# Backward pass of a pre-LN decode block: a thirteenth 8 KiB tile, twelve kept V, the activation's row form, and gK in the light iteration

## The chip, the cores and the metric

The kernel runs on one core of a Trainium2 chip. The metric is the device time of one execution in microseconds. Engines are called PE (matrix products, with PEld for its weight loads), DVE (VectorE), ACT (ScalarE), POOL (GpSimd) and SP (SyncE, which here only issues DMAs). All DMAs of the core share 16 DMA engines.

## The reference

One decode step (one token) of a block with attention over a cache and a ReLU MLP, and the gradients of all its inputs for a given gradient of the output:

```python
def _A_ref(x, k_cache, v_cache, wq, wo):          # B=2, Sq=1, D=640, H=32, Sk=4096, Dh=128
    q = (x @ wq).reshape(B, Sq, H, Dh).transpose(0, 2, 1, 3)
    scores = jnp.einsum("bhqd,bhkd->bhqk", q, k_cache) * (Dh ** -0.5)
    p = softmax(scores)
    o = jnp.einsum("bhqk,bhkd->bhqd", p, v_cache)
    return o.transpose(0, 2, 1, 3).reshape(B, Sq, H * Dh) @ wo

def _B_ref(x, w1, w2):                            # Dff=1728
    return jnp.maximum(x @ w1, 0) @ w2

h  = x + _A_ref(layernorm(x), k_cache, v_cache, wq, wo)
h2 = h + _B_ref(layernorm(h), w1, w2)
_out, _vjp = jax.vjp(f, A_x, A_k_cache, A_v_cache, A_wq, A_wo, B_w1, B_w2)
return (_out, *_vjp(grad_out))
```

All arrays are bf16. K and V caches are 2 x 32 heads of 4096 x 128, 1 MiB each, so 128 MiB are read at least once, and the gradients of both caches, another 128 MiB, are written.

## The kernel before

A head's K or V is one tile of 128 x 32 x 128 bf16, 8 KiB in each partition. Twelve such tiles (NBIG, L80) live in one pool; each belongs for the time being to a use: `ld` (loads), `g` (outputs gK and gV), `f` (weight gradients), `q` (weights and rows of the end). `take` and `give` (L94 to L117) hand them out and back, `share` (L123) says how many each use should own, and `more_home` adds tiles when other pools are released.

**First pass** (`p1_iter`, L448). Iteration i works on three heads at once: the scores of head i (K transposed in four groups by `pair_transpose`, L418, then `pair_matvec`, L431), the softmax of head i-1 and its product with K (`pk`, two halves, DVE), and the product of that with V of head i-2 (`m_part`). An iteration has eight parts, k = 0 to 7, and between them other work is let in. The row maximum `rmax` is made by DVE in part 6 and used by PE in part 1 of the next iteration. Transposed groups land in `t_sb`, five buffers.

**Second pass** (`p2_iter`, L836). Turn j works on one head: V is transposed again and multiplied with the output's gradient, and two outer products are written out: gV (from `rb` and the copy `pp` of P) and gK (from `rb` and `gsp`). Both are 1 MiB, made by DVE in two halves (`outer_half`, L815; in some turns ACT makes the last eight columns of gV) and issued by POOL. gK of turn j-1 is made at the beginning of turn j. V is read a second time (`Wt`), except for heads that keep theirs: KEPT = (6, 5), six in the first batch and five in the second.

**Order.** The plan (from L1062) runs first-pass iterations alone up to i = 40; from P2_AT = 41 a second-pass turn starts with every other iteration. I call an iteration in which a turn starts heavy and the one after it light. Parts of the turn are let in after parts 1 (two of them), 3, 4 and 6 of the heavy iteration (MIXED, L1112), and the turn's last part after part 1 of the light one (REST, L1113). After the first pass the turns run alone (j = 12 and up). Loads are queued in the order of the plan and issued by SP as soon as an `ld` tile is free (`pump`).

**Background.** Three lists of generators are let in at rates: the middle of a batch (`middle_gen`, L719: sum over wo, LayerNorm, w1, the gradient of the MLP, then `go_group`, whose products over wo give each head's output gradient), the weight gradients (`fin_gen`, L939, by `outer_rows`, L910), and the gradient of x (`gx_gen`, L953). In the middle of the second batch, L753 to L760 compute the activation a second time from w1 with rows in another order (`arow`, row p of column cf is p*13 + cf), which `mlp_out` (L694) needs for its loads of w2. Products with accumulation over a row (`ttr`, L641) write a `junk` tile. `bcast_cols` (L615) turns columns into rows that are equal in all partitions: `gbc`, `fbc`, `hbc`. `store_row` (L633) writes the two small outputs through `orow`, two buffers.

The first loads, `xr` from A_x and grad_out, are issued by SP (L210, L211), then five tiles of wq (L378), then K and V.

Of the kernel before, what the change touches and what calls it, by code (L numbers as in the profile page):

```python
# [15 lines left out]
def kernel(  # L16
# [20 lines left out]
    nc = tc.nc  # L37
# [18 lines left out]
    NMT = (32, 12)  # L56
# [23 lines left out]
    NBIG = 12  # L80
# [76 lines left out]
    sel = const.tile([128, 2, 2, 64], BF16)  # L157
    nc.gpsimd.memset(sel[:], 0.0)
    for par in range(2):
        nc.gpsimd.affine_select(out=sel[:, par, :, :], in_=sel[:, par, :, :], compare_op=ALU.not_equal,  # L160
                                fill=1.0, base=-par, pattern=[[0, 2], [-2, 64]], channel_multiplier=1)
# [17 lines left out]
    xr = cols.tile([4 * ND, 128], BF16)  # L179
# [15 lines left out]

    gom = cols.tile([128, H, B, 2, 2], BF16)
# [3 lines left out]
    Uc = cols.tile([128, B, H], FP32)  # L200
# [3 lines left out]
    P_bf = cols.tile([128, B * H, NSC], BF16)  # L204
# [5 lines left out]
    nc.sync.dma_start(out=xr[0:2 * ND, :], in_=A_x.rearrange("b s (c p) -> (b s c) p", p=128))  # L210
    nc.sync.dma_start(out=xr[2 * ND:4 * ND, :], in_=grad_out.rearrange("b s (c p) -> (b s c) p", p=128))  # L211
# [11 lines left out]
    def ln_fwd(xs, nb, xh, rstd):  # L223

        def st(name, dt=FP32):
            return small.tile([128, nb], dt, tag=f"ln_{name}{nb}", bufs=1, name=f"ln_{name}")
# [7 lines left out]
        cent = small.tile([128, nb, ND], FP32, tag=f"ln_cent{nb}", bufs=1, name="ln_cent")  # L234
        nc.vector.tensor_tensor(out=cent[:], in0=xs, in1=bc(mean[:], ND), op=ALU.subtract)
        sq = small.tile([128, nb, ND], FP32, tag=f"ln_sq{nb}", bufs=1, name="ln_sq")
# [5 lines left out]
        y_bf = small.tile([128, nb, ND], BF16, tag=f"ln_y{nb}", bufs=1, name="ln_y")  # L242
# [33 lines left out]
    def ln_bwd(gh, xh, rstd, add, dst, nb):  # L276

        def t3(name):
            return small.tile([128, nb, ND], FP32, tag=f"lb_{name}{nb}", bufs=1, name=f"lb_{name}")
# [35 lines left out]
    nc.tensor.transpose(x_ps[:], xr[:], ident_bf[0:4 * ND, 0:4 * ND])  # L315
# [18 lines left out]
    def pair_rows(dst, src, hs, bs):  # L334

        n, nb = hs.stop - hs.start, bs.stop - bs.start
        t = pst([128, 2, n, nb], FP32, "mid", "pr_ps")
        for par in range(2):
            nc.tensor.matmul(t[:, par, :, :], lhsT=sel[:, par, :, :].rearrange("p c k -> p (c k)"),
                             rhs=src[:, hs, bs], start=True, stop=True)  # L340
        for c in range(2):
            rows = slice(64 * c, 64 * c + 64)
            for par in range(2):
                nc.vector.tensor_copy(out=dst[rows, hs, bs, par, c], in_=t[rows, par, :, :])
# [26 lines left out]
    def all_q():  # L371

        zero = small.tile([128, H * B], BF16, tag="zero", bufs=1, name="zero")
        nc.vector.memset(zero[:], 0.0)
# [7 lines left out]
        nc.tensor.matmul(q_ps[:].rearrange("p h b -> p (h b)"), lhsT=ident_bf[:], rhs=zero[:], start=True, stop=False)  # L382
# [12 lines left out]
    KEPT = (6, 5)  # L395
# [4 lines left out]
    u4 = cols.tile([128, 128], FP32)  # L400
# [14 lines left out]
    def pair_transpose(nat, g, dve=False, busy=0):  # L415
# [8 lines left out]
        t_sb = mats.tile([128, GT // 2, 128], FP32, tag="XT", bufs=5, name="t_sb")  # L424
# [24 lines left out]
    def p1_iter(i, dve_group, busy):  # L449
# [48 lines left out]
        if p is not None:  # L498

            bp, hp = pairs[i - 1]  # L500
            bhp = bp * H + hp
# [41 lines left out]
        if p is not None:  # L543
# [3 lines left out]
            (nc.gpsimd if i < P2_AT else nc.vector).tensor_copy(out=P_bf[:, bhp, :], in_=ep[:, :, 0])  # L547
# [60 lines left out]
    def u_out(b):  # L608

        t = pst([128, H], FP32, "mid", "uc_ps")  # L610
        nc.tensor.matmul(t[:], lhsT=u4[:], rhs=fold[:], start=True, stop=True)
        nc.vector.tensor_tensor(out=Uc[:, b, :], in0=t[:], in1=rt[:, b, :], op=ALU.mult)


    def bcast_cols(colsrc, n, kc_of, dst):  # L615

        for c0 in range(0, n, 4):
            t = pst([128, 512], FP32, "bc", "bc_ps")
            w = 0
            for c in range(c0, min(n, c0 + 4)):  # L620
# [4 lines left out]
            nc.scalar.copy(out=dst[:, c0 * 128:c0 * 128 + w], in_=t[:, 0:w])  # L625
            yield
# [6 lines left out]
    def store_row(col_bf, n, dst):  # L633
# [3 lines left out]
        r = small.tile([16, 128], BF16, tag="orow", bufs=2, name="orow")  # L637
# [3 lines left out]
    def ttr(in0, in1, acc, width, kc=128, junk=None):  # L641
        if junk is None:
            junk = cols.tile([128, D], BF16, tag="junk", name="junk")
# [14 lines left out]
    def go_group(b, h0, h1, hbc):  # L658
# [4 lines left out]
        for k in range(n):  # L663
            yield from turn()
            ttr(wo_t[:, h0 + k, :], hbc[:], go32[:, k:k + 1], D)
# [16 lines left out]
        nc.vector.tensor_tensor(out=ud[:, 0:n], in0=Uc[:, b, hs], in1=negdot[:, hs, b], op=ALU.mult)  # L682
# [8 lines left out]
    def mlp_out():  # L691
# [3 lines left out]
        for k in range(NW2):  # L695
            while free["q"] < 1:
                yield
# [21 lines left out]
    def middle_gen(b):  # L719
        if o_next[0] < (b + 1) * H // OG:  # L720
            o_group()
        nc.vector.tensor_reduce(out=u4[:], in_=u_bank[0][:].rearrange("p (s d) -> p d s", s=4),
# [28 lines left out]
        if b == B - 1:  # L751
            ar_ps = pst([128, NFF, B], FP32, "mid", "ar_ps")
            for cf in range(NFF):  # L753
                for c in range(ND):
                    nc.tensor.matmul(ar_ps[:, cf, :], lhsT=w1_t[:, c, bass.ds(cf, 128, step=NFF)],
                                     rhs=x2c[:, c, :], start=(c == 0), stop=(c == ND - 1))
                yield 0.25
            nc.vector.tensor_scalar(out=arow[:, 0:NFF, :], in0=ar_ps[:], scalar1=0.0, scalar2=None, op0=ALU.max)
            if F_rem:
                nc.vector.tensor_copy(out=arow[:, NFF, :], in_=acol[:, NFF, :])  # L760
# [4 lines left out]
        fbc = cols.tile([128, Dff], BF16, tag="fbc", name="fbc")  # L765
        gx2 = small.tile([128, 1, ND], FP32, tag="gx2", bufs=1, name="gx2")
        gx2p = small.tile([128, ND, 3], FP32, tag="gx2p", bufs=1, name="gx2p")
        FW = Dff // 3
        spread_f = bcast_cols(one(ghfc, b), NF, f_kc, fbc)
        have = 0  # L770
        for k in range(3):
            while have < min(Dff, (k + 1) * FW):
                next(spread_f)
                have += 512
                yield
            for c in range(ND):
                yield from turn()
                ttr(w1_t[:, c, k * FW:(k + 1) * FW], fbc[:, k * FW:(k + 1) * FW], gx2p[:, c, k:k + 1], FW)
# [4 lines left out]
        hbc = cols.tile([128, D], BF16, tag="rowbc", name="hbc")  # L783
        yield from bcast_cols(one(gh1c, b), ND, lambda c: 128, hbc)
# [10 lines left out]
    def ga_gen():  # L795

        gbc = cols.tile([128, Dff], BF16, tag="fbc", name="gbc")
        for b in range(B):
            yield from bcast_cols(one(gc, b), ND, lambda c: 128, gbc[:, b * D:(b + 1) * D])
        for k in range(NW2):  # L800
# [3 lines left out]
            for c in range(k * FP, min(NF, (k + 1) * FP)):  # L804
                kc = f_kc(c)
                for b in range(B):
                    yield from turn()
                    ttr(t[0:kc, c - k * FP, :], gbc[0:kc, b * D:(b + 1) * D], ga[0:kc, b, c:c + 1], D, kc)
# [14 lines left out]

    def p2_iter(j, busy, act=0):

        c = S2[j] if j < NP1 else None
        p = S2[j - 1] if j >= 1 else None
        if p is not None:
            bp, hp = turns[j - 1]
            pair_matvec(p["dp"], p.pop("T3"), 3, gom[:, hp, bp, :, :])  # L830
            gsp = small.tile([128, NSC, 2], BF16, tag="gsp", name="gsp")
            nc.vector.scalar_tensor_tensor(  # L832
                out=gsp[:], in0=p["dp"][:, :, None].to_broadcast([128, NSC, 2]), scalar=negdot[:, hp, bp:bp + 1],
                in1=P_bf[:, bp * H + hp, :, None].to_broadcast([128, NSC, 2]), op0=ALU.add, op1=ALU.mult)
        if c is not None:
# [9 lines left out]
            rb = mats.tile([128, 256], BF16, tag="rb", bufs=4, name="rb")  # L845
            nc.scalar.activation(out=rb[:], in_=bank[:, 128:384], func=ACT.Copy, scale=rt[:, b, h:h + 1])  # L846
            pp = small.tile([128, NSC, 2], BF16, tag="pp", name="pp")
            nc.gpsimd.tensor_copy(out=pp[:], in_=P_bf[:, b * H + h, :, None].to_broadcast([128, NSC, 2]))
# [391 lines left out]
```

## Time and profile before

| what | value |
|---|---|
| median of 3 runs | 902.24 us (900.63 to 907.04) |
| profiled execution, span | 902.8 us |
| PE, PEld busy | 757.2, 634.2 us |
| DVE, ACT, POOL busy | 687.2, 485.8, 198.7 us |
| moved by DMA | 362.89 MB, mean 402 GB/s |
| HBM read, written | 212.16 MB, 149.13 MB |
| loads of K, V, V again (Wt) | 64, 64, 53 of 1 MiB |
| first pass alone, both, second pass alone | 0 to about 258, to 452, to the end |

The profile comes from one execution. Its span is cut into 40 slices of 22.6 us; a digit is the busy share in tenths. The DMA row is the share of time in which the 16 engines have a packet in work, GB/s what they moved; PEclk is the clock that was granted to PE, in tenths of full speed. In a table by stretches, each engine has its busy time and in brackets its instructions. A line of the timeline gives start, duration, engine, source line, and in brackets how long the engine was idle before it and what ended that.

### The profile page before, as it was taken

To read this page: it belongs to the slowest core of one execution; us is meant where nothing else is said; L and a number is where in the kernel's file an instruction comes from. 1 tells how busy PE (TensorE), PEld (TensorE's weight loads), DVE (VectorE), ACT (ScalarE), POOL (GpSimd) and SP (SyncE) were. 2 spreads that over 40 slices of the span, in tenths; PEclk is the share of its full clock that TensorE was granted. 3 is DMA by queue.
4 is the path that set the end of the run, shared out by engine and by line. 5 is a ranking of instruction groups with operands and counts; after the bars stand their busy time and mean duration, and the time that the engine had idled before them with its cause. 6 is when DMAs were issued, how large, how long until landed. Compare 5 with 4: busy or idle time off the path is not lost.

```text
span 902.8 us, 24701 instructions
## 1 busy us (share of the span) xinstructions
PE 757.2 (84%) x10205; PEld 634.2 (70%) x10205; DVE 687.2 (76%) x1286; ACT 485.8 (54%) x1248; POOL 198.7 (22%) x349
## 2 busy tenths in 40 slices
PE   3999899899999898898968876878999778959880
PEld 3888788888888787787757765656767566645560
DVE  2566788777988796697778697769798448999982
ACT  0444344344565554464536677776577656637660
POOL 1344444343311011010012141122112111111120
PEclk9999999999999999798985555555557555555555
DMA  8999999999879999999999999999999999999995
GB/s 365 426 419 414 417 402 417 424 424 377 330 310 381 415 405 424 425 416 425 404 399 399 389 410 417 417 389 388 404 413 409 425 424 424 419 425 422 423 422 240
DMA packets 56256, 362.89 MB, mean 402 GB/s; under 512 B 5680, under 2 KB 11696, under 8 KB 15312
## 3 DMA queue, kind: packets, MB, share of 16 engines
q1 hardware_dynamic: 34704, 212.18, 57.8%
q0 software_dynamic: 18432, 134.23, 35.9%
q10 hardware_dynamic: 3008, 14.91, 4.1%
q8 instruction: 80, 1.31, 0.5%
q14 instruction: 32, 0.26, 0.1%
HBM read 212.16 MB, written 149.13 MB: 400 GB/s over the span
## 4 chain that ended last, share of the span: by engine, by line
PE 49%; DMA 21%; DVE 13%; ACT 11%; issue 5%; SPq 1%; POOL 0%; ACTq 0%; POOLq 0%; DVEq 0%
PE t_ps L423 21%; PE m_ps L457 10%; DMA Vt<-in_A_v_cache_dram 10%; ACT t_sb L428 3%; ACT gV L880 3%; DMA out_dram<-gK 3%; PE s_ps L436 3%; DVE gV L819 3%; PE u_ps L486 3%; PE dp_ps L436 3%; PE o_ps L928 3%; DMA wqs<-in_A_wq_dram 3%; DVE pk L464 2%; DVE gK L819 2%; DMA Kt<-in_A_k_cache_dram 2%
## 5 line engine op out<-in xcount | busy, mean ns | idle before, releaser
L428 ACT COPY t_sb<-t_ps 128x512 f32<-128x512 f32 x479 | 273.4, 585 | 211.0 <-PE t_ps L423 205.2
L436 PEld LDWEIGHTS <-t_sb 128*128 128x128 bf16 x4096 | 181.6, 103 | 62.0 <-ACT t_sb L428 27.4
L423 PE MATMUL t_ps<-ident_f,Wt 128*128 128x128 f32 x848 | 207.2, 396 | 0.4 <-ACT t_sb L428 0.4
L457 PE MATMUL m_ps<-pk,Vt 128*128 128x129 bf16 x2048 | 171.8, 223 | 16.1 <-DMA Vt<-in_A_v_cache_dram 14.7
L464 DVE TENSOR_TENSOR pk<-Kt,ep 128x2048 bf16<-128x2048 bf16 x128 | 156.5, 1223 | 33.5 <-PE m_ps L457 15.3
L423 PEld LDWEIGHTS t_ps<-ident_f,Wt 128*128 128x128 f32 x848 | 144.1, 206 | 33.2 <-issue 27.1
L819 DVE TENSOR_TENSOR gK<-rb,gsp 128x2048 bf16<-128x2048 bf16 x128 | 152.2, 1223 | 13.1 <-DMA out_dram<-gV 10.9
L423 PE MATMUL t_ps<-ident_f,Kt 128*128 128x128 f32 x1024 | 156.7, 287 | 4.4 <-DMA Kt<-in_A_k_cache_dram 4.3
L457 PEld LDWEIGHTS <-Vt 128*128 128x128 bf16 x2048 | 125.3, 99 | 46.5 <-issue 29.7
L819 DVE TENSOR_TENSOR gV<-rb,pp 128x2048 bf16<-128x2048 bf16 (+1 forms) x128 | 142.9, 1140 | 10.9 <-DMA out_dram<-gK 6.0
L423 PEld LDWEIGHTS t_ps<-ident_f,Kt 128*128 128x128 f32 x1024 | 113.7, 145 | 8.5 <-PE s_ps L436 2.6
L474 POOL COPY pk<-ep 128x16 bf16<-128x16 bf16 x80 | 83.2, 1042 | 161.0 <-ACT ep L512 90.5
L436 PE MATMUL dp_ps<-gom,t_sb 128*128 128x2 bf16 x2048 | 96.6, 168 | 17.8 <-ACT t_sb L428 17.1
L881 POOL DMA_DIRECT2D out_dram<-gV x64 | 34.2, 534 | 304.7 <-DVE gV L819 175.4
L436 PE MATMUL s_ps<-qm,t_sb 128*128 128x2 bf16 x2048 | 87.7, 164 | 1.2 <-DVE t_sb L426 1.2
L860 POOL DMA_DIRECT2D out_dram<-gK x64 | 34.0, 532 | 222.0 <-DVE gK L819 167.9
L571 ACT CAST MT<-m_ps 128x128 bf16<-128x128 f32 x64 | 17.1, 267 | 104.4 <-PE m_ps L457 104.3
L934 ACT CAST ot<-o_ps 128x512 bf16<-128x512 f32 (+4 forms) x160 | 70.2, 489 | 2.9 <-DMA out_dram<-ot 1.5
L832 DVE SCALAR_TENSOR_TENSOR gsp<-dp_ps,negdot,P_bf 128x64 bf16<-128x64 f32 x64 | 18.0, 282 | 50.8 <-PE dp_ps L436 50.0
L644 DVE CUSTOM_DVE_ANT_0 junk<-wo_t,hbc 128x640 bf16<-128x640 bf16 x64 | 52.7, 823 | 0.2
L846 ACT ACTIVATE rb<-dp_ps,rt 128x256 bf16<-128x256 f32 x64 | 30.1, 470 | 41.1 <-PE dp_ps L841 40.4
L644 DVE CUSTOM_DVE_ANT_0 gxj<-wqs,gqr 128x1024 bf16<-128x1024 bf16 x40 | 48.8, 1220 | 1.5 <-DMA wqs<-in_A_wq_dram 1.3
(200 smaller groups left out, 779.0 us busy)
## 6 DMA issues: line engine op xcount, KB each, us to landing
Kt<-in_A_k_cache_dram SPq DMA_DIRECT2D x64, 1024.0 KB, 15.3
Vt<-in_A_v_cache_dram SPq DMA_DIRECT2D x64, 1024.0 KB, 15.3
out_dram<-gV POOLq DMA_DIRECT2D x64, 1024.0 KB, 13.1
out_dram<-gK POOLq DMA_DIRECT2D x64, 1024.0 KB, 13.9
Wt<-in_A_v_cache_dram SPq DMA_DIRECT2D x53, 1024.0 KB, 12.4
wq_t<-in_A_wq_dram SPq DMA_DIRECT2D x5, 1024.0 KB, 9.0
wo_t<-in_A_wo_dram SPq DMA_DIRECT2D x4, 1280.0 KB, 18.1
wqs<-in_A_wq_dram SPq DMA_DIRECT2D x5, 1024.0 KB, 17.1
```

The source lines that it names most:

```text
L423: nc.tensor.transpose(t_ps[:, j, :], natf[:, 2 * cc:2 * cc + 2, :].rearrange("p c k -> p (c k)"), ident_f[:])
L428: nc.scalar.copy(out=t_sb[:], in_=t_ps[:])
L436: nc.tensor.matmul(dst[:, sc:sc + 2], lhsT=v[:, j, :, par], rhs=vecs[:, par, :], start=(par == 0), stop=(par == 1))
L457: nc.tensor.matmul(r["m"][:, 0:129], lhsT=r["V"][:, sc, :], rhs=r["pk"][sc // HALF][:, sc % HALF, 0:129], start=(sc == 0), stop=(sc == NSC ...
L464: nc.vector.tensor_tensor(out=p["pk"][k][:, :, 0:128].rearrange("p s (a two) -> p s a two", two=2), in0=p["K"][:, sl, :].rearrange("p s (a ...
L474: nc.gpsimd.tensor_copy(out=col, in_=e)
L644: nc.vector.tensor_tensor_reduce(out=junk[0:kc, 0:width], in0=in0, in1=in1, scale=1.0, scalar=0.0, op0=ALU.mult, op1=ALU.add, accum_out=acc)
L819: nc.vector.tensor_tensor(out=pairs_view(dst[:, sl, :]), in0=row.rearrange("p (a two) -> p a two", two=2)[:, None, :, :].to_broadcast([128 ...
L846: nc.scalar.activation(out=rb[:], in_=bank[:, 128:384], func=ACT.Copy, scale=rt[:, b, h:h + 1])
L860: nc.gpsimd.dma_start(out=natural(out_2, bp, hp), in_=gK[:])
L881: nc.gpsimd.dma_start(out=natural(out_3, b, h), in_=gV[:])
L934: nc.scalar.copy(out=ot[0:P, k, n0:n0 + nn], in_=o_ps[0:P, 0:nn])
```

## The change

- NBIG is 13. The space comes from smaller buffers: P in 52 slots that are reused (`P_slot`), three rows of 640 (`rows`) in place of `xr`, `junk`, `fbc`, `gbc`, `hbc`, `zero`, `u4`, ten second-kind slots for M instead of twelve, `sel` without its doubled half, LayerNorm tiles shared by both sizes, and one buffer fewer for `t_sb` (4), `rb` (3), `pp`, `gsp` (2) and `orow` (1).
- KEPT is (6, 6). Shares of `ld` grow by one.
- gK of a turn is made in its light iteration by `p2_tail`, as long as both passes run.
- `arow` is made in `fin_gen` from the row form of the activation, by 13 small products with the identity; `mlp_out` waits for it. The gradient of w2 (out_7) is laid out by 128 rows of 13, and a rest of 64.
- The rows of the MLP's gradient come in parts of 640, 640 and 448 instead of three of 576.
- `xr` is loaded by ACT's queue.
- While the rows for the gradient of x are spread, the weight gradients go on at 0.4 of their rate.

```diff
-    NMT = (32, 12)
+    NMT = (32, 10)
-    NBIG = 12
+    NBIG = 13
-    xr = cols.tile([4 * ND, 128], BF16)
+    rows = cols.tile([128, 3, D], BF16)
+    junk_row = rows[:, 2, :]
-    P_bf = cols.tile([128, B * H, NSC], BF16)
+    NPS = 52
+    P_bf = cols.tile([128, NPS, NSC], BF16)
+    P_free = list(range(NPS))
+    P_slot = {}
-    nc.sync.dma_start(out=xr[0:2 * ND, :], ...
+    xr = rows[0:4 * ND, 0, 0:128]
+    nc.scalar.dma_start(out=xr[0:2 * ND, :], ...
...
-            nc.tensor.matmul(t[:, par, :, :], lhsT=sel[:, par, :, :].rearrange("p c k -> p (c k)"),
-                             rhs=src[:, hs, bs], start=True, stop=True)
+            for c in range(2):
+                nc.tensor.matmul(t[64 * c:64 * c + 64, par, :, :], lhsT=sel[:, par, :],
+                                 rhs=src[:, hs, bs], start=True, stop=True)
...
-    KEPT = (6, 5)
+    KEPT = (6, 6)
-    u4 = cols.tile([128, 128], FP32)
+    u4 = junk_row[:, 0:256].bitcast(FP32)
-        t_sb = mats.tile([128, GT // 2, 128], FP32, tag="XT", bufs=5, name="t_sb")
+        t_sb = mats.tile([128, GT // 2, 128], FP32, tag="XT", bufs=4, name="t_sb")
...
-        r = small.tile([16, 128], BF16, tag="orow", bufs=2, name="orow")
+        r = small.tile([16, 128], BF16, tag="orow", bufs=1, name="orow")
...
-            while free["q"] < 1:
-                yield
+            while free["q"] < 1 or "arow" not in FIN:
+                yield 0.0 if "arow" not in FIN else 0.5
...
-        if b == B - 1:
-            ar_ps = pst([128, NFF, B], FP32, "mid", "ar_ps")
-            for cf in range(NFF):
-                for c in range(ND):
-                    nc.tensor.matmul(ar_ps[:, cf, :], lhsT=w1_t[:, c, bass.ds(cf, 128, step=NFF)],
-                                     rhs=x2c[:, c, :], start=(c == 0), stop=(c == ND - 1))
-                yield 0.25
-            nc.vector.tensor_scalar(out=arow[:, 0:NFF, :], in0=ar_ps[:], scalar1=0.0, scalar2=None, op0=ALU.max)
-            if F_rem:
-                nc.vector.tensor_copy(out=arow[:, NFF, :], in_=acol[:, NFF, :])
...
+    def p2_gs(j):
+        p = S2[j]
+        bp, hp = turns[j]
+        pair_matvec(p["dp"], p.pop("T3"), 3, gom[:, hp, bp, :, :])
+        gsp = small.tile([128, NSC, 2], BF16, tag="gsp", bufs=2, name="gsp")
+        nc.vector.scalar_tensor_tensor(...)
+        P_free.append(P_slot.pop((bp, hp)))
+        return gsp
...
-        p = S2[j - 1] if j >= 1 else None
+        p = S2.get(j - 1)
...
+    def p2_tail(j):
+        p = S2[j]
+        bp, hp = turns[j]
+        gsp = p2_gs(j)
+        yield
+        gK = take("g", [128, NSC, 128], "gK")
+        outer_half(gK, p["rb"][:, 128:256], gsp, 0)
+        yield
+        outer_half(gK, p["rb"][:, 128:256], gsp, 1)
+        nc.gpsimd.dma_start(out=natural(out_2, bp, hp), in_=gK[:])
+        give(gK)
+        del S2[j]
+        yield
...
-        yield from outer_rows(FIN["ar"], Dff, FIN["gr"], D, out_7, Dff // 96)
+        yield
+        ar_ps = pst([128, NFF, B], FP32, "mid", "ar_ps")
+        for cf in range(NFF):
+            nc.tensor.matmul(ar_ps[:, cf, :], lhsT=FIN["ar"][0:B, bass.ds(cf, 128, step=NFF)],
+                             rhs=ident_bf[0:B, 0:B], start=True, stop=True)
+        nc.scalar.copy(out=arow[:, 0:NFF, :], in_=ar_ps[:])
+        nc.scalar.copy(out=arow[:, NFF, :], in_=acol[:, NFF, :])
+        FIN["arow"] = True
+        yield
+        yield from outer_rows(FIN["ar"], NFF * 128, FIN["gr"], D, out_7, NFF, F_rem)
...
-    REST = {1: 1}
+    REST = {1: 2, 4: 1, 6: 1}
+    def p2_whole(j):
+        yield from p2_iter(j, 0)
+        yield from p2_tail(j)
...
-            share(ld=8 + 3 * more, g=7 + 3 * more)
+            share(ld=9 + 3 * more, g=7 + 3 * more)
...
-            share(ld=5 + more, g=5 + 2 * more, f=3, q=2 + 3 * more)
+            share(ld=6 + more, g=5 + 2 * more, f=3, q=2 + 3 * more)
...
-            g2 = p2_iter(j, 0, 8 if i is None and j <= H else 0)
+            if i is not None and n + 1 < len(plan) and plan[n + 1][1] is None:
+                g2 = p2_whole(j)
+            else:
+                g2 = p2_iter(j, 0, 8 if i is None and j <= H else 0)
...
-                bg_step(1, RATE2)
+                bg_step(1, RATE2 * (0.4 if spreading[0] else 1.0))
```

## The prediction

> **What bounds the kernel now.** I read first the slices of the page, for the DMA engines and the granted clock:
>
> ```profile
> PEclk9999999999999999798985555555557555555555
> DMA  8999999999879999999999999999999999999995
> GB/s 365 426 419 414 417 402 417 424 424 377 330 310 381 415 405 424 425 416 425 404 399 399 389 410 417 417 389 388 404 413 409 425 424 424 419 425 422 423 422 240
> ```
>
> The DMA engines are busy nearly everywhere, and no slice moves more than 426 GB/s. I take 424 GB/s as full rate. The page's 362.89 MB would need 856 us at it, so about 47 us of the 902.8 us span are lost service, and only less data or less loss can shorten the kernel. Where it is lost, by stretches:
>
> ```profile
> 20.00:200.00 180.00, 171.81 (x2915) 151.25 (x2916) 132.35 (x242) 73.79 (x220) 74.14 (x92) 1.00 1.02 418
> 200.00:280.00 80.00, 77.01 (x1362) 68.06 (x1360) 65.24 (x170) 43.00 (x118) 18.22 (x33) 1.00 0.88 347
> 280.00:320.00 40.00, 36.01 (x579) 31.46 (x577) 32.73 (x68) 22.20 (x65) 5.25 (x8) 0.96 1.00 397
> 320.00:440.00 120.00, 107.61 (x1692) 94.47 (x1693) 91.70 (x183) 62.99 (x175) 12.87 (x21) 0.90 1.01 422
> 440.00:540.00 100.00, 77.74 (x1004) 68.99 (x1003) 79.68 (x149) 59.75 (x159) 23.63 (x46) 0.63 1.00 397
> 540.00:700.00 160.00, 132.63 (x1207) 105.66 (x1206) 128.30 (x234) 114.36 (x288) 32.57 (x71) 0.55 1.00 405
> 700.00:880.00 180.00, 146.47 (x1275) 107.52 (x1273) 145.76 (x200) 107.26 (x227) 27.34 (x59) 0.54 1.01 423
> 880.00:903.00 23.00, 1.33 (x25) 0.92 (x22) 6.15 (x7) 1.17 (x2) 1.59 (x3) 0.56 0.57 239
> ```
>
> Columns: stretch, its length, busy time of PE, its weight loads, DVE, ACT, POOL, granted clock, DMA share, GB/s. Lost against 424: 14.5 us in 200 to 280 (80 x 77/424), 2.5 in 280 to 320, 6.4 in 440 to 540, 7.2 in 540 to 700, 10 in the tail, some 6 elsewhere. From 700 to 880 nothing is lost: there time is bytes alone, so whatever the engines win earlier counts only as bytes moved before 700.
>
> In 200 to 280 it is the engines that hold DMA back: all 32 first-batch heads are done, VectorE (65.2 of 80 us busy) carries the products of the middle on top of each head, and PE waits for data for only 2.5 us between 205 and 325 (the waits). Two heads with one backward turn I call a pair. One that DMA does not delay looks like this, light iteration first, then heavy:
>
> ```profile
> 328.10:334.70 6.60, 6.60 (x107) 5.61 (x104) 6.57 (x14) 4.37 (x14) 1.71 (x2) 1.00 1.01 421
> 334.70:342.90 8.20, 7.62 (x143) 6.74 (x143) 6.37 (x13) 4.65 (x12) 0.53 (x1) 1.00 1.01 426
> ```
>
> The light one is bound by DVE (6.57 of 6.6), the heavy one by PE (7.62 of 8.2). A pair moves four tiles of K and V, one reloaded V and two outputs, 7 x 1.049 MB = 7.34 MB, 17.3 us at full rate; the first six pairs use kept V and move 6.29 MB, 14.8 us.
>
> **The change, step by step**, against the profiled span of 902.8 us (the median of three runs is 902.24, inside 900.63 to 907.04, so the differences carry over).
>
> One V fewer is reloaded: 53 loads of Wt become 52, 1.05 MB/424 = 2.5 us. It was read in a stretch that drains at full rate later, so I count all of it: -2.5 (bounds -2.5 and 0).
>
> The thirteenth tile: while the engines bind (200 to 280) loads run one tile further ahead, and when DMA binds after 325 one tile is already there: 1.05 MB again, -2.5. Bounds: 0, if the tile only fills with an idle V, and -5.0, if the lead is won a second time in 440 to 700, where 13.6 us are lost. From the 60th head on the extra kept V holds it, which the first term has paid.
>
> xr and grad_out move from SP's queue to ACT's. The first wq load was issued at 1.53 us, behind two issues that began at 0.74: -0.8, since SP issues all twelve loads of the start back to back. ACT loads its table from 0.73 to 2.01 us; should its DMAs stand behind that, x arrives some 1.3 us later, which the wq tiles hide (PE waits for wq at 11.4 anyway). Bounds -0.8 and +1.3.
>
> gK in the light iteration: gsp and two halves of gK (0.28 + 2 x 1.22 = 2.7 us of DVE), the last four transposes' products (0.4 us of PE) and one POOL issue move from the heavy to the light iteration, half a pair earlier. No instruction is added. The first outputs start some 7 us earlier, in a stretch where DMA is 0.80 to 0.88 busy: half a tile of lead on average, -1.2 (0 to -2.5). Against it, heavy falls to about 7.7 us (PE), and light grows to 6.6 + 1.5 = 8.1 us with gK's second half falling behind the next maximum, or 9.3 with both in front. I take 8.1, since the second half is issued after the maximum: a pair of 15.8 us. The first six pairs took 96.2 us (257.7 to 353.9), 16.0 each, DMA waits included; the later five 17.9. So 0; bounds -1 (six pairs at 15.8) and +6 (six pairs at 17.0). The 17.3 us of DMA covers the later ones.
>
> The second layout of the MLP activation: 65 matmuls over w1 and their wait leave the middle of batch two. They show as this DVE gap:
>
> ```profile
> 494.72 1.83 DVE L819 TENSOR_TENSOR gV<-rb,pp 128x2048 bf16<-128x2048 bf16 x2
> 502.35 0.18 DVE L758 TENSOR_SCALAR arow<-ar_ps 128x26 bf16<-128x26 f32 x1 [5.81 <-PE ar_ps L755]
> ```
>
> 5.8 us of DVE disappear; instead come 13 small matmuls and two ACT copies in the gradient's background work. DMA falls to 384 GB/s in 500 to 520 (1.9 us lost), so I take -1.9; bounds -5.8 and 0 (a wait for output tiles follows at 504 anyway). out_7 with 128 rows needs 28 pieces for 36: 8 x 0.49 us of ACT, which is 46 us idle in 540 to 700: 0 (to -3.9).
>
> One row buffer for two in store_row. The second copy now waits until the first row has left, and DVE stands:
>
> ```profile
> 804.58 0.21 DVE L638 COPY orow<-row_ps 5x128 bf16<-5x128 bf16 x1
> 804.81 1.26 SPq L639 DMA_DIRECT2D out_dram<-orow  x2
> 805.14 0.21 DVE L638 COPY orow<-row_ps 5x128 bf16<-5x128 bf16 x1 [0.36 <-PE row_ps L636]
> ```
>
> The packets of these rows start 4.8 to 11.0 us after the issue, behind reads, so DVE stands about 7 us, and behind it wait gsp, gK and gV of that turn and the gx products. DMA lives on what is queued, 4.7 MB issued and not yet moved at 805, 11 us, and DVE has 7.1 us free in 800 to 880. I take +0.7, bounds 0 and +7. The Trainium skill ("DMA: Bandwidth & Descriptors", Anatomy of one DMA) gives about 2.0 us fixed cost for a small DMA; by it the term would be 0. The trace, with its queue in front, is what I use.
>
> At nothing: t_sb with 4 buffers, since with gK moved every transpose stands behind the products of the fourth one before it in PE's own order; were gK not moved, the T3 of a turn would be held over the pair. rb 3, gsp 2, pp 2: their last readers are issued earlier on the same in-order engine. The P slots, the shared rows and halved statistics save space; one more ACT copy of 0.4 us per batch. pair_rows gets 24 matmuls of 0.17 us, in turns that wait for ACT or DMA.
>
> Sum: -2.5 -2.5 -0.8 -1.2 -1.9 +0.7 = -8.2: a span of 894.6, a time of 894.0.
>
> **Rivals.** *The lead pays more than once.* For it: 440 to 700 loses 13.6 us with queues that run dry between outputs, and 280 to 320 another 2.5. A third of these 16.1 us back besides: 894.0 - 5.4 = 888.6. Against it: PE there never waits for a reloaded V, and DVE waits for output tiles instead, of which there are no more than before. 0.25.
>
> *The lead is absorbed*: the heavier light iteration and the row wait eat it at their bounds short of that (+6, +1): 901. 0.10.
>
> *Slower: the two iterations no longer overlap and PE's clock halves in the light one.* Before, each was near both limits; now heavy waits for PE and light for DVE, once per iteration through the maximum that DVE hands to PE. Two rows show what waiting does:
>
> ```profile
> 367.50:371.00 3.50, 1.29 (x9) 0.95 (x9) 1.29 (x9) 1.07 (x2) 0.00 (x0) 0.94 1.03 433
> 371.00:375.00 4.00, 3.17 (x34) 3.11 (x35) 2.12 (x3) 1.08 (x3) 0.00 (x0) 0.50 1.01 426
> ```
>
> At half clock four transposes take 1.05 us for 0.62 (x4), eight products with V 1.05 for 0.63 (x4), u 0.98 for 0.62: +3.8 us on some 5.9 us of PE, so light is 9.7 to 10.9 us and a pair 17.4 to 18.6. That decides once light passes 17.3 - 7.7 = 9.6 us. Price: six pairs at +1.4 to +2.6 and five at up to +0.7, and no lead from tile or gK: up to 19 us, 14 as the middle; 902.2 - 2.5 - 0.8 - 1.9 + 0.7 + 14 = 912. Against it: in 334.7 to 342.9 PE kept full clock with 7.62 of 8.2 busy. 0.20. The Trainium skill ("TensorE: Matmul & The Clock Gate", Part 1) says the clock drops after an idle window of about 3.4 us; the two rows agree (1.29 of 3.5 busy, then 0.50), and by it the gaps of 2 us in a light iteration would not suffice, which leaves this rival without its second half.
>
> **Numbers.** Forecast 894.0 with 0.45, its own range 889 to 899. About 1% (9 us) is what a measurement can tell from no change: below 893.2 is faster, above 911.3 slower. Half the forecast's case lies below 893.2 (0.225), with the first rival 0.475: faster 0.48. Slower 0.20, same 0.32. Range 885 (the lead's rival with its bounds) to 908 (absorbed, with the row wait at +7): it leaves out the slower rival.
>
> **What would show it.** Right: 52 Wt loads and 361.8 MB; 200 to 320 above 375 GB/s; no DVE gap for arow, 500 to 520 above 395; pairs at 15 to 16 us before the first reload; first wq issue near 0.75; a DVE wait for an orow DMA of 4 to 11 us. Wrong: pairs above 17.3 us with clock 0.5 inside them, DMA below 400 in 320 to 440, new waits of ACT for t_sb products, or a queue that is empty after the row wait.

## The result, and the profile after

The changed kernel takes 909.64 us (median of 20 runs, 906.27 to 914.35), the kernel before 903.63 us in the same series (20 runs). The ratio is 1.0062, with a 95% interval of 1.0045 to 1.008: about 6 us slower, where 8 us less were forecast, and 1.6 us beyond the upper end of the range. The profiled execution has a span of 905.4 us.

The slices of the changed kernel's page, in the same 40 parts as before (granted clock, busy share of the DMA engines, what they moved):

```profile
PEclk9999998999999999998985555555555655555555
DMA  9999999999989999999999999999999999999977
GB/s 378 419 410 405 410 397 410 420 418 408 355 304 363 423 421 423 422 422 425 389 408 392 419 418 415 398 423 406 419 423 381 382 426 424 425 399 364 410 311 318
```

Two long places stand out against the slices before, and a short one (the 31st and 32nd slice, 679 to 724 us, with 381 and 382 for 409 and 425). From the second slice to the ninth the DMA row is full, but moves 397 to 420 GB/s, where seven of these eight had 414 to 426 before. And from the 36th slice on (792 us) it falls to 311 at the lowest, where before it stayed at 422 or more until the last slice. By stretches, with the last 205 us cut once more (columns as before: busy PE, weight loads, DVE, ACT, POOL, clock, DMA share, GB/s):

```profile
20.00:200.00 180.00, 171.18 (x2868) 149.90 (x2867) 130.68 (x238) 73.39 (x219) 72.27 (x91) 0.98 1.02 411
200.00:280.00 80.00, 75.97 (x1337) 66.94 (x1330) 64.72 (x169) 41.67 (x115) 19.36 (x34) 1.00 0.90 350
280.00:320.00 40.00, 36.57 (x639) 32.17 (x637) 33.45 (x66) 23.15 (x63) 3.15 (x7) 1.00 1.01 419
320.00:440.00 120.00, 105.57 (x1727) 92.82 (x1724) 92.73 (x190) 65.31 (x178) 9.18 (x21) 0.96 1.01 423
440.00:540.00 100.00, 74.54 (x952) 65.84 (x951) 82.96 (x160) 61.76 (x164) 23.13 (x48) 0.65 1.00 403
540.00:700.00 160.00, 125.92 (x1178) 100.22 (x1177) 122.57 (x217) 107.90 (x269) 34.24 (x68) 0.53 1.01 409
700.00:780.00 80.00, 68.50 (x621) 50.90 (x620) 64.22 (x83) 49.57 (x108) 11.95 (x26) 0.56 1.01 413
780.00:880.00 100.00, 71.05 (x567) 49.17 (x567) 76.10 (x113) 52.30 (x112) 14.21 (x31) 0.53 0.93 377
880.00:905.00 25.00, 13.72 (x126) 9.84 (x125) 12.47 (x13) 9.79 (x19) 3.39 (x8) 0.57 0.82 331
```

Between 200 and 700 us the change does what it was to do: each of the five stretches moves 1 to 22 GB/s more than before. On both sides of it something is lost: 20 to 200 has 411 for 418 (3.0 us: 180 x 7/424), 700 to 780 has 413 for 424 (2.1 us), and 780 to 880 has 377 for 422 (10.6 us). The two last stretches of the kernel before, for comparison:

```profile
700.00:780.00 80.00, 66.41 (x592) 49.31 (x591) 54.35 (x67) 48.13 (x105) 10.93 (x24) 0.52 1.01 424
780.00:880.00 100.00, 80.06 (x684) 58.21 (x682) 91.42 (x134) 59.13 (x123) 16.41 (x35) 0.56 1.01 422
```

The times of second-pass turns say the same. Turn 0 makes its rows `rb` at 259.9 us (before 257.7, so 2.2 us late), turn 52 at 778.6 (before 782.1, 3.5 us early), and the end comes 2.6 us late.

What happens at 790 us is in the timeline of DVE (start, duration, line, operation, count, and in brackets the idle time before it and what ended it):

```profile
788.24 1.22 DVE L653 CUSTOM_DVE_ANT_0 rows<-wqs,gqr 128x1024 bf16<-128x1024 bf16 x1
...
789.39 0.21 DVE L647 COPY orow<-row_ps 5x128 bf16<-5x128 bf16 x1
804.80 0.21 DVE L647 COPY orow<-row_ps 5x128 bf16<-5x128 bf16 x1 [15.21 <-DMA out_dram<-orow]
804.94 0.26 DVE L829 SCALAR_TENSOR_TENSOR gsp<-dp_ps,negdot,P_bf 128x64 bf16<-128x64 f32 x1
```

It is the wait that the prediction named, for the single row buffer, but 15.2 us long. What it does to DMA shows in the finer stretches of the changed kernel (same columns):

```profile
790.00:805.00 15.00, 6.12 (x53) 4.41 (x53) 0.20 (x2) 4.18 (x10) 0.00 (x0) 0.50 1.01 427
805.00:820.00 15.00, 11.01 (x124) 9.86 (x124) 14.90 (x22) 8.55 (x21) 2.00 (x4) 0.65 0.97 383
820.00:860.00 40.00, 27.78 (x211) 18.51 (x208) 39.59 (x60) 21.93 (x45) 7.06 (x15) 0.53 0.97 383
860.00:880.00 20.00, 18.86 (x135) 11.80 (x134) 11.96 (x16) 13.53 (x27) 3.04 (x8) 0.50 0.74 300
```

While DVE stands (0.20 us busy of 15) DMA loses nothing: 427 GB/s, out of what was queued. Afterwards DVE has almost no free time until 860 (14.90 of 15, 39.59 of 40), and DMA moves 383 GB/s. Bytes issued and not yet moved, added up from the trace's issues and packets, were 6.5 MB at 790 us and 0.76 MB at 805: the queue was used up while DVE, which makes the large outputs, stood.

Not only the outputs stood. SP issues the rows and the loads in one order, and the second row could not be issued before its copy. The timeline of SP (a line spans from the first of its issues to the end of the last):

```profile
789.62 15.71 SPq L648 DMA_DIRECT2D out_dram<-orow  x2
805.38 0.44 SPq L1008 DMA_DIRECT2D wqs<-in_A_wq_dram  x1
805.91 25.21 SPq L450 DMA_DIRECT2D Wt<-in_A_v_cache_dram  x4
```

Two loads of 1 MiB follow the second row within 0.6 us. So for 15 us neither POOL (which waits for gK) nor SP put anything large into the queue; ACT issued one output.

### The profile page after: what moved, and what is told of

Same layout as the page of the kernel before. It is cut to its first block, busy times and chain, and to the rows that moved or that the text cites. A ratio compares the mean times of both kernels' runs of the same rounds, so it can differ in the third digit from the quotient of the medians.

```text
span 905.4 us, 24731 instructions
## 1 busy us (share of the span) xinstructions
PE 750.9 (83%) x10169; PEld 625.2 (69%) x10169; DVE 685.8 (76%) x1284; ACT 486.7 (54%) x1244; POOL 193.8 (21%) x349
## 2 busy tenths in 40 slices
DMA packets 56288, 361.84 MB, mean 400 GB/s; under 512 B 5680, under 2 KB 11888, under 8 KB 15472
## 4 chain that ended last, share of the span: by engine, by line
PE 40%; DVE 22%; DMA 18%; ACT 10%; issue 7%; SPq 0%; ACTq 0%; POOL 0%; POOLq 0%; DVEq 0%
PE t_ps L429 18%; DMA Vt<-in_A_v_cache_dram 9%; PE m_ps L463 8%; DVE rows L653 7%; DVE gV L818 5%; DVE gK L818 5%; ACT gV L887 4%; DMA Kt<-in_A_k_cache_dram 4%; DVE pk L470 3%; ACT t_sb L434 3%; PE s_ps L442 3%; PE o_ps L955 2%; PE dp_ps L442 2%; PE u_ps L492 2%; DMA out_dram<-gV 2%
## 5 line engine op out<-in xcount | busy, mean ns | idle before, releaser
L434 ACT COPY t_sb<-t_ps 128x512 f32<-128x512 f32 x479 | 274.0, 588 | 204.6 <-PE t_ps L429 200.8
L429 PE MATMUL t_ps<-ident_f,Wt 128*128 128x128 f32 x832 | 202.7, 395 | 0.8 <-ACT t_sb L434 0.8
L470 DVE TENSOR_TENSOR pk<-Kt,ep 128x2048 bf16<-128x2048 bf16 x128 | 156.3, 1222 | 44.4 <-ACT ep L517 21.1
L429 PEld LDWEIGHTS t_ps<-ident_f,Wt 128*128 128x128 f32 x832 | 141.2, 206 | 32.5 <-issue 23.7
L961 ACT CAST ot<-o_ps 128x512 bf16<-128x512 f32 (+3 forms) x152 | 68.3, 490 | 5.5 <-ACT ot L961 1.9
L867 POOL DMA_DIRECT2D out_dram<-gK x53 | 28.3, 533 | 164.0 <-DVE gK L818 146.9
L653 DVE CUSTOM_DVE_ANT_0 rows<-wo_t,rows 128x640 bf16<-128x640 bf16 x64 | 52.6, 822 | 0.4 <-ACT rows L633 0.2
L653 DVE CUSTOM_DVE_ANT_0 rows<-wqs,gqr 128x1024 bf16<-128x1024 bf16 x40 | 48.8, 1220 | 0.2
```

Source lines behind the costliest of these rows:

```text
L429: nc.tensor.transpose(t_ps[:, j, :], natf[:, 2 * cc:2 * cc + 2, :].rearrange("p c k -> p (c k)"), ident_f[:])
L434: nc.scalar.copy(out=t_sb[:], in_=t_ps[:])
L470: nc.vector.tensor_tensor(out=p["pk"][k][:, :, 0:128].rearrange("p s (a two) -> p s a two", two=2), in0=p["K"][:, sl, :].rearrange("p s (a ...
L653: nc.vector.tensor_tensor_reduce(out=junk[0:kc, 0:width], in0=in0, in1=in1, scale=1.0, scalar=0.0, op0=ALU.mult, op1=ALU.add, accum_out=acc)
L961: nc.scalar.copy(out=ot[0:kp, k, n0:n0 + nn], in_=o_ps[0:kp, 0:nn])
```

## The experiments

Every kernel ran beside the kernel before on the same chip; ratios are to that, with 95% intervals. Differences between single profiles carry less than the ratios: the stretch from 200 to 280 us came out at 329 to 350 GB/s among kernels that hardly differ there (up to 4 us).

### The four output rows get places of their own

The changed kernel, where the rows no longer share one buffer but lie side by side in the junk row, which has room:

```diff
+    stored = [0]
-        r = small.tile([16, 128], BF16, tag="orow", bufs=1, name="orow")
+        r = junk_row[0:16, 128 * stored[0]:128 * stored[0] + 128]
+        stored[0] += 1
```

> The changed kernel, with the four small output rows each in a place of its own in the junk row, so that no row waits for another's DMA. Theory W (the single row buffer made the loss): the 15.2 us in which DVE stands before the second row are gone, DMA stays above 420 GB/s from 780 to 880, and the time is 898 to 902, below the kernel before (903.6). Rival L (the loss comes from the light iteration, from the t_sb buffers or from the extra kept V): the time stays at 906 to 910.

Measured: 899.3 us, ratio 0.995 (0.9926 to 0.9975). Against the changed kernel that is 1.12% less, 10.1 us. The same finer stretches of this kernel:

```profile
790.00:805.00 15.00, 10.82 (x101) 7.43 (x100) 14.22 (x22) 7.96 (x23) 1.98 (x4) 0.59 1.01 426
805.00:820.00 15.00, 11.43 (x131) 7.90 (x128) 14.90 (x21) 10.56 (x23) 2.93 (x6) 0.75 1.02 425
820.00:860.00 40.00, 28.97 (x226) 19.85 (x225) 35.68 (x54) 22.27 (x45) 6.96 (x15) 0.50 1.01 424
860.00:880.00 20.00, 18.49 (x121) 10.65 (x120) 11.28 (x14) 12.97 (x25) 2.66 (x7) 0.50 1.01 421
```

The wait is gone (DVE 14.22 of 15), SP goes on to issue `wqs` at 796.57 us and `Wt` at 802.40, and DMA holds 421 GB/s or more to 880 us. So the wait cost 10 us, more than the change as a whole lost. How much of it came through DVE's outputs and how much through SP's loads was not separated.

### The kernel before with one row buffer

```diff
-        r = small.tile([16, 128], BF16, tag="orow", bufs=2, name="orow")
+        r = small.tile([16, 128], BF16, tag="orow", bufs=1, name="orow")
```

> The kernel before, with one row buffer instead of two and nothing else changed. Theory W: DVE stands 10 to 15 us between the first two rows and the time goes up by 6 to 11 us, to 910 to 915. Rival L: within 2 us of 903.6, because the queued DMA work covers the wait.

Measured: 907.99 us, ratio 1.004 (1.0014 to 1.0066), 3.6 us (1.3 to 6.0). The middle lies between the theory's 6 to 11 us and the rival's 2, and the interval reaches to both. The timeline of DVE in this kernel:

```profile
809.05 0.21 DVE L638 COPY orow<-row_ps 5x128 bf16<-5x128 bf16 x1
820.61 0.21 DVE L638 COPY orow<-row_ps 5x128 bf16<-5x128 bf16 x1 [11.35 <-DMA out_dram<-orow]
```

The same wait, 11.35 us, without any other part of the change, and again a loss from 780 to 880 (395 GB/s for 422). It costs a third of what it does in the changed kernel. Two things differ there, a wait 4 us longer and a DVE that is then full for 55 us; which of them makes the difference was not separated.

How long a row waits can be read from the trace's records of its packets (issue to the start of the row's last packet) beside the bytes queued at about that time:

```
kernel               row issued   queued    at 424 GB/s   last packet after
before, first row    804.81 us    4.7 MB    11.2 us        7.0 us
before, second row   805.38 us    4.7 MB    11.2 us       10.4 us
after                789.62 us    6.5 MB    15.3 us       14.1 us
after, at 256 bytes  788.66 us    6.4 MB    15.0 us       14.4 us
before, one row      809.29 us    4.1 MB     9.7 us       10.4 us
own places, first    795.67 us    7.0 MB    16.5 us       11.1 us
own places, second   796.23 us    7.0 MB    16.5 us       15.8 us
```

(Queued is at the nearest of the marks 5 us apart; where two rows follow each other closely, the earlier five of the ten packets are taken for the first.) In five of the seven the last packet comes within 1.2 us of the time that the queue in front needs. The two rows of the profile before lay behind 4.7 MB; in the changed kernel the row comes 15 us earlier, behind 6.5 MB. Its last two rows, issued at 868.8 and 876.0 us when DMA had fallen to 300 GB/s, were through after 1.6 us each.

### gK in the light iteration, alone

The kernel before, with gK of a turn made by `p2_tail` in its light iteration, and nothing else:

```diff
+    def p2_tail(j):
...
-    REST = {1: 1}
+    REST = {1: 2, 4: 1, 6: 1}
...
+            if i is not None and n + 1 < len(plan) and plan[n + 1][1] is None:
+                g2 = p2_whole(j)
```

> The kernel before, with gK in the light iteration as the only change. The prediction's step (outputs half a pair earlier): -1.2, so 901 to 904. Rival L (light bound by DVE, heavy by PE, no overlap): pairs before the first reload go from 16.0 to 17 us and the time to 908 or more.

Measured: 903.41 us, ratio 0.9994 (0.9966 to 1.0023). Neither a gain of 1.2 us nor none can be told from it; a loss of the size that the slower rival needs (14 us) can be excluded.

### The activation's second layout from row form, alone

The kernel before, with `arow` from 13 products with the identity and out_7 laid out by 128 rows:

```diff
-            for cf in range(NFF):
-                for c in range(ND):
-                    nc.tensor.matmul(ar_ps[:, cf, :], lhsT=w1_t[:, c, bass.ds(cf, 128, step=NFF)],
...
+        for cf in range(NFF):
+            nc.tensor.matmul(ar_ps[:, cf, :], lhsT=FIN["ar"][0:B, bass.ds(cf, 128, step=NFF)],
+                             rhs=ident_bf[0:B, 0:B], start=True, stop=True)
...
+        yield from outer_rows(FIN["ar"], NFF * 128, FIN["gr"], D, out_7, NFF, F_rem)
```

> The kernel before, with the activation's second layout made from the row form (and out_7 by 128 rows) as the only change. The prediction's step: the 5.8 us DVE gap near 500 us is gone and the time falls by 1.9, to 901 to 902.5. Rival: the wait for output tiles that follows takes it back, 903 to 904.

Measured: 901.19 us, ratio 0.9958 (0.9933 to 0.9983): 3.8 us gained (1.5 to 6.1), twice the term of 1.9 in the middle; the interval has the term in it and passes its bound of 5.8 only just. In its profile 440 to 540 has 407 GB/s for 397 and 540 to 700 has 412 for 405 (2.4 and 2.6 us); 700 to 780 gives 3.4 back (406 for 424), and some 4 come after 880. These are readings of single profiles: 200 to 320 us, where the edit changes nothing, differs by 3.4 us the other way (337 and 381 GB/s for 347 and 397). The second stretch was counted at 0, with out_7's fewer pieces costing ACT less only where ACT is idle anyway.

### The tiles start at a multiple of 256 bytes

With own rows the kernel still read slowly from 20 to 200 us (411 GB/s). The trace's packet records show where. Nine tenths of the bytes of that stretch are packets of 8192 bytes, each one row of K, V or a weight; before, such a packet took 309 ns from the 10th to the 90th percentile, in the changed kernel 309 to 320, 312 in the middle. What is read there is the same; where the tiles lie differs. As built, the big tiles start at byte 47616 of each partition before, a multiple of 256, and at 39840 after, 160 bytes past one, since all that was made smaller lies below them. The next kernel is the one with own places for the rows (its tiles start at 39584, 160 past as well), with 96 bytes of padding, which puts them at 39680:

```diff
-    half_f32c = const.tile([128, 1], FP32)
-    nc.vector.memset(half_f32c[:], 0.5)
-    half_f32 = half_f32c[:].to_broadcast([128, 128])
+    half_f32c = const.tile([128, 32], FP32)
+    nc.vector.memset(half_f32c[:, 0:1], 0.5)
+    half_f32 = half_f32c[:, 0:1].to_broadcast([128, 128])
```

> The kernel of e1 with 96 unused bytes in each partition ahead of the big tiles, so that these start at a multiple of 256 bytes again (they start 160 bytes past one in e1 and in the changed kernel, and at a multiple before). Theory A (start address): reads of 8 KiB rows take 309 ns each again in 20 to 200 us (311 to 321 in e1), 20:100 and 100:200 move 418 GB/s instead of 411, and the time falls by 3 to 4 us below e1, to 0.991 of the kernel before. Rival R (another cause, such as the load of xr by ACT or thirteen tiles in flight): rows and rates stay as in e1, time 0.995.

Measured: 893.49 us, ratio 0.9877 (0.9844 to 0.991), faster than both kernels. Its stretches up to 440 us:

```profile
20.00:200.00 180.00, 170.55 (x2924) 149.38 (x2924) 132.72 (x240) 73.19 (x219) 74.85 (x93) 0.99 1.02 419
200.00:280.00 80.00, 75.99 (x1335) 67.20 (x1332) 63.95 (x168) 42.37 (x117) 17.71 (x31) 1.00 0.89 344
280.00:320.00 40.00, 35.76 (x605) 31.14 (x602) 34.51 (x69) 23.78 (x65) 3.14 (x7) 1.00 1.01 422
320.00:440.00 120.00, 104.80 (x1727) 91.52 (x1728) 94.00 (x197) 65.78 (x179) 9.91 (x23) 0.98 1.01 424
```

The engines' work is the same, and the first stretch moves 419 GB/s. The interval lies wholly below that of the kernel with own rows alone (0.9926 to 0.9975): 96 unused bytes are worth 0.73%, 6.6 us, where 3 to 4 were expected. The stretch from 20 to 200 us accounts for 3.4 of them (180 x 8/424); where the others arise was not shown. It is not the engines' own speed: DVE's products `pk` and gK take 1222 and 1225 ns in this kernel, 1221 and 1224 with own rows alone.

The opposite, on the kernel before: 32 bytes of padding, so that its tiles start 32 past a multiple of 256 (the same edit with 16 elements).

> The kernel before with 32 unused bytes ahead of the big tiles, nothing else changed, so that they start 32 bytes past a multiple of 256. Theory A: rows of 8 KiB take 311 to 321 ns in 20 to 200 us, the rate falls from 418 to 411, time up by 2 to 4 us (1.002 to 1.005). Rival R: 309 ns, 418 GB/s, 1.000.

Measured: 912.64 us, ratio 1.0081 (1.0046 to 1.0116), 7.3 us where 2 to 4 were expected. The row from 20 to 200 us:

```profile
20.00:200.00 180.00, 173.10 (x2848) 152.53 (x2848) 129.74 (x240) 73.38 (x219) 70.76 (x90) 0.98 1.02 410
```

So 32 bytes alone make the kernel before as slow as the whole change did. And how coarse the boundary is, by the kernel with own rows and tiles 128 bytes past a multiple of 256 (64 elements):

> The kernel of e1 with 224 unused bytes, big tiles 128 past a multiple of 256 (a multiple of 64 and 128). If only a multiple of 256 is good, rows take 311 to 321 ns and 411 GB/s as in e1; if 64 or 128 is enough, 309 ns and 418 GB/s.

A single run: 900.62 us, and

```profile
20.00:200.00 180.00, 168.92 (x2868) 147.49 (x2868) 131.09 (x238) 73.11 (x219) 73.42 (x91) 0.99 1.02 411
```

The reads stay slow: half of 256 does not help. The last of this group is the changed kernel with the padding and with its single row buffer:

> The changed kernel with 96 bytes of padding and nothing else, so that its 8 KiB tiles start at a multiple of 256 bytes (39936); the single row buffer stays. Theory (row wait and tile start are two separate losses): the wait of DVE for the first output row stays at 12 to 16 us, 8 KiB rows take 309 ns, 20 to 200 us goes back to 418 GB/s or more, and the ratio is 1.0062 - 0.0073 = 0.999 (902 to 904 us). Rival (what reads win earlier is lost again while DVE stands, since the queue only gets shorter): the ratio stays at 1.004 to 1.006 although the rows take 309 ns.

Measured: 904.5 us, ratio 0.9991 (0.9968 to 1.0013), as the first theory has it. Its two stretches that matter:

```profile
20.00:200.00 180.00, 169.42 (x2870) 147.87 (x2870) 131.02 (x238) 73.10 (x219) 73.41 (x91) 0.98 1.02 419
...
780.00:880.00 100.00, 71.77 (x574) 50.41 (x574) 75.14 (x110) 52.79 (x112) 14.03 (x30) 0.53 0.94 384
```

The early reads are back at 419, the row wait (15.4 us) and its loss stay. The two losses add: padding alone takes off 0.71%, own rows alone 1.12%, together 1.83%, and both in one kernel took off 1.85%.

### What the tile and the kept V are worth

The best kernel with five V kept in the second batch, thirteen tiles as they are:

```diff
-    KEPT = (6, 6)
+    KEPT = (6, 5)
```

> The kernel of e5 with KEPT (6, 5), so 53 reloads of V and a thirteenth tile that is free for loads. The prediction's first term: one reload more costs 2.5 us against e5. Rival: the reload falls into stretches where the engines bind, and the time is within 1 us of e5.

Measured: 895.33 us, ratio 0.989 (0.9858 to 0.9923). The intervals overlap nearly whole: 0.13%, 1.2 us by the ratios, against a term of 2.5, is not resolved. From 700 to 780 us this kernel moves 423 GB/s, and so does the next, while all five with six kept V and the slower rate have 413 or 414 (1.9 us); this would speak for a kept V that gives back part of what it saves. But from 780 to 880 the kernel with five kept moves 406 GB/s for 421 (3.5 us the other way), and these are single profiles, so it stays open. Then also without the tile:

```diff
-    NBIG = 13
+    NBIG = 12
-    KEPT = (6, 6)
+    KEPT = (6, 5)
...
-            share(ld=9 + 3 * more, g=7 + 3 * more)
+            share(ld=8 + 3 * more, g=7 + 3 * more)
...
-            share(ld=6 + more, g=5 + 2 * more, f=3, q=2 + 3 * more)
+            share(ld=5 + more, g=5 + 2 * more, f=3, q=2 + 3 * more)
```

> As e5, but twelve tiles, five V kept in the second batch and the old shares: all of the change but the tile and the V it keeps. Theory (the terms as predicted, 2.5 us for the lead and 2.5 us for the V): 5 us more than e5, a ratio near 0.993; against e8, which has thirteen tiles and five kept V, 2.5 us more, 0.9915 to 0.992. Rival (the tile is worth only the V it holds): 0.989, as e8, with the stretch from 200 to 280 us as in e8.

Measured: 898.58 us, ratio 0.9939 (0.9913 to 0.9965). The tile and the V it keeps are worth 0.62%, 5.6 us, where 5.0 was expected; the two intervals just part. How the sum divides between lead and kept V stays open, since the kernel between them overlaps with both.

### The weight gradients at full rate

700 to 780 us lost 10 GB/s in the changed kernel and in the best one, which let the weight gradients go on at 0.4 of their rate while the rows for the gradient of x are spread:

```diff
-                bg_step(1, RATE2 * (0.4 if spreading[0] else 1.0))
+                bg_step(1, RATE2)
```

> As e5, but the weight gradients keep their full rate while the rows for the gradient of x are spread. Theory (the slower rate leaves DMA short of outputs from 700 to 780 us, 414 GB/s in the changed kernel against 424): 700 to 780 comes back to 420 GB/s or more and the time falls by 1 to 2 us, ratio 0.986. Rival (with full rate these products and copies come ahead of the gradient of x, whose rows then end later): 700 to 780 gains, 780 to 880 loses as much, ratio 0.987 to 0.990.

Measured: 897.32 us, ratio 0.9906 (0.987 to 0.9941), no gain, and

```profile
700.00:780.00 80.00, 71.63 (x624) 52.37 (x623) 58.67 (x76) 51.50 (x116) 11.09 (x24) 0.52 0.98 397
780.00:880.00 100.00, 77.10 (x689) 56.53 (x687) 91.30 (x130) 58.54 (x120) 18.08 (x37) 0.60 1.01 424
```

The theory is wrong, and the rival is wrong in the place: at full rate DVE does less from 700 to 780 (58.67 us, at the slower rate 65.11 in the best kernel) and more afterwards, and DMA falls to 397 in the first of the two. The slower rate pays, if anything; the intervals overlap.

## Why the prediction was wrong, step by step

**The step that failed: one row buffer, +0.7 us (0 to +7).** The wait and its mechanism were named, its size was not right: 10.1 us. Two parts of the working broke.

The length, "about 7 us", was taken from packets that started 4.8 to 11.0 us after their issue. The buffer is free only when the last packet has gone; in the profile before that was 7.0 us for the first row, but 10.4 us for the second. More important, the row is late because of what is queued in front. "4.7 MB issued and not yet moved, 11 us" stood in the prediction, but as the cover for the wait. It is the wait's own length: the longer the queue that should cover, the longer DVE stands, and when it may go on, the queue is nearly empty (6.5 to 0.76 MB).

The cover, "7.1 us free in 800 to 880", was free time of DVE in the profile before. It did not cover 15.2 us. That SP's loads stand behind the second row as well was not in the working at all. And DVE, which makes the outputs that fill the queue, then ran without a gap to 860 us with DMA at 383. "A queue that is empty after the row wait" was in the list of what would make the prediction wrong, and it is what the trace shows. The fixed cost of about 2.0 us that the Trainium skill gives ("DMA: Bandwidth & Descriptors", Anatomy of one DMA), there for a DMA that GpSimd issues while these rows are issued by SP, was rightly set aside; behind a filled queue the rows took 7.0 to 15.8 us to their last packet, and only the two late ones, with little in front, took 1.6.

**The step that was missing: "at nothing ... save space", measured at 6.4 us** (0.71%; 6.6 with own rows). What the smaller buffers do to the place of the big tiles was not asked. With the row term (10.1 for 0.7) this is 9.4 + 6.4 = 15.8 us more than forecast. The forecast as a ratio is 894.0/902.24 = 0.9909, the measured one 1.0062, 13.8 us apart; the other 2 us would be gains that came out larger, which the intervals do not resolve.

**The gains came out near their sum, in part by luck.** With both losses taken out the ratio is 0.9877 (0.9844 to 0.991), 11.1 us (8.1 to 14.1); the forecast without its row term has 8.9. That the sum fits says little of its terms: one was twice as large in the middle, one was not resolved, and one was not measured alone. Single terms:

- Tile and kept V, -2.5 and -2.5: together -5.6. Loads of `Wt` 52, 361.84 MB, as stated. That 200 to 320 would stand above 375 GB/s was too much: 373 ((350 x 80 + 419 x 40)/120).
- First loads, -0.8: the first wq load is issued at 0.74 us instead of 1.53, as stated. What that is worth was not measured alone.
- Row form of the activation, -1.9 (-5.8 to 0): -3.8 alone. 500 to 520 moves 420 GB/s (before 384), and DVE's gap is gone. The timeline of DVE in the changed kernel at the same place of the middle, where 5.81 us stood before:

```profile
492.03 0.28 DVE L829 SCALAR_TENSOR_TENSOR gsp<-dp_ps,negdot,P_bf 128x64 bf16<-128x64 f32 x1 [1.66 <-PE dp_ps L442]
492.35 2.36 DVE L818 TENSOR_TENSOR gK<-rb,gsp 128x2048 bf16<-128x2048 bf16 x2
494.62 0.17 DVE L756 TENSOR_SCALAR acol<-hf_ps 128x13 bf16<-128x13 f32 x1
...
498.30 0.28 DVE L829 SCALAR_TENSOR_TENSOR gsp<-dp_ps,negdot,P_bf 128x64 bf16<-128x64 f32 x1 [1.27 <-PE dp_ps L442]
```

  DVE goes on with gK and the first layout `acol`, and waits 1.66 us at most. A share in 540 to 700, which the term left out, shows in single profiles only.
- gK in the light iteration, -1.2: not resolved, 0.9994 with an interval of 0.28% to each side. That the heavier light iteration costs nothing was right: six pairs took 94.3 us (259.9 to 354.2), 15.7 each where 15.8 was taken. One such pair in the changed kernel, light first, then heavy:

```profile
329.80:337.20 7.40, 7.01 (x116) 5.90 (x113) 7.40 (x12) 4.96 (x15) 0.53 (x1) 1.00 1.01 423
337.20:345.40 8.20, 7.17 (x134) 6.46 (x135) 5.43 (x14) 4.32 (x11) 0.78 (x2) 1.00 1.01 423
```

DVE is full in the light one (7.40 of 7.40, 8.1 was taken) and has time left in the heavy one (5.43 of 8.20), and the clock is 1.00 in both.

Of the savings "at nothing", four `t_sb` buffers for five show no cost: no wait of ACT for the readers of `t_sb` appears, and the waits of ACT for PE's transposes sum to 200.8 us (before 205.2).

**The rivals.** The slower one gave 912 us, near what came, for a reason that did not occur: the clock from 320 to 440 rose from 0.90 to 0.96, and pairs did not lengthen. What the prediction held against its clock was wrong, though: PE is busy for 1.29 of the 3.5 us at 367.5, so that stretch is not idle, and gaps of 2 us can bring the clock down. In the trace of the kernel before the clock fell from full to half five times up to 466.2 us; in the 3.4 us ahead of each fall PE was busy for 0.89 to 1.59 us, and its longest idle time there was 1.45 to 2.15 us. "Absorbed, with the row wait at +7" at 908 was nearest in mechanism; it had the row wait, and no slower reads. Its own terms give 906.3 and not 908, since the +7 stands in place of the +0.7. That the lead pays more than once (888.6) is not shown: the best kernel, at 0.9877 x 902.24 = 891.1 us, needs no more than the forecast's own terms without the row and with the larger one for `arow` (894.0 - 0.7 - 1.9 = 891.4).

## What to carry to other kernels

Before a buffer is cut to one, ask what its DMA is queued behind: this kernel lives on a full DMA queue, its small output waited about as long as that queue lasted, and the engine that waited, with the loads issued behind it, came back to an empty one. When small buffers shrink, look where the large ones now start: a shift of 32 bytes cost this kernel 0.8%, and a few bytes of padding gave it back. And if a change mixes gains with savings "at nothing", undo the savings first: here the gains were worth 1.2%, and two of the savings cost 1.8%.

## What the runs showed of the hardware

**A row's start in SBUF changes the time of its read packet.** Rows of 8192 bytes, 20 to 200 us, where the DMA engines only read; packet times from the traces' records:

```
start of the tiles past     kernel                packet, mean    10th, 50th, 90th      GB/s
a multiple of 256 bytes                                           percentile
  0                         before                311.9 ns        309, 309, 309         418
  0                         after + 96 bytes      311.4 ns        309, 309, 309         419
  0                         own rows + 96 bytes   311.5 ns        309, 309, 309         419
 32                         before + 32 bytes     317.4 ns        313, 313, 320         410
128                         own rows + 224 bytes  316.0 ns        309, 312, 320         411
160                         after                 316.7 ns        309, 312, 320         411
160                         own rows              316.5 ns        309, 312, 320         411
```

The Trainium skill ("DMA: Bandwidth & Descriptors", How a descriptor splits into AXI transactions) says of a descriptor that starts off a 256-byte boundary that its first transaction starts at the boundary below, and that the bytes in between are fetched unused and still cost beats. The runs agree in kind: of the four starts tried, only the multiple of 256 was fast. By beats of 32 bytes, as the Trainium skill counts them there, the estimate for a start 32 past would be 257 for 256 beats, 0.4%, and for 160 past 261, 2%; measured were 1.8% (317.4 for 311.9) and 1.7% (316.7 for 311.4), so the cost does not grow with the distance. By transactions it would be 33 for 32, an estimate of 3%. The Trainium skill speaks there of reading from such an address; here the odd address is the one in SBUF that is written to. From 700 to 780 us, where reads and outputs share the engines, packets of both kinds have a median of 309 ns with either start, so the loss is shown clearly only where reads run alone. That accounts for about half of what the kernels lost (3.4 of 6.6 and 7.3 us).
